# Windowed attention with sinks, then a normalised two-layer network: the first layer's Strassen half from the fourth chunk on, and a new order of loads

## The chip, the cores and the metric

The kernel runs on one core of one Trainium2 chip. The metric is the device time of one execution in microseconds, as the median of several runs. A profiled execution has a span, from its first to its last instruction, and a time of its own, which is a little longer.

## What is computed

Four sequences of 768 positions with 8 heads of 64 go through attention in which a position sees the first 4 positions (sinks) and the last 128 positions. The result, 512 values for each position, is normalised, goes through two matrix products with a relu between them, and is added to the result of the attention.

```
scores = q @ k.T / sqrt(64)                      # batch 4, heads 8, seq 768, head_dim 64
keep   = (pos_k < 4) | (0 <= pos_q - pos_k < 128)
a      = softmax(where(keep, scores, -1e9))
x      = (a @ v) heads side by side              # [4, 768, 512]
xn     = (x - mean(x)) / sqrt(var(x) + 1e-6) * g_ln
out    = x + relu(xn @ w_ch1) @ w_ch2            # w_ch1 512 x 2048, w_ch2 2048 x 512
```

## The kernel before

The 3072 positions are cut into 24 tiles of 128 (t) and 12 chunks of two tiles (c); three chunks make a sequence. Weights and activations are held in bf16, sums in fp32.

Nothing is ordered by hand. `Plan` collects operations (`P.op(name, engines, priority, ...)`), each with its possible engines and an assumed duration, what it reads and writes, and a priority that reads as a due time: the smaller goes first. `Plan.run` is a list scheduler: it takes the engine on which something can start first, and of the operations that can start there within a small window (0.2 to 0.25 us) the one of the smallest priority. `nb` is a time before which an operation does not start. Operations of TensorE with a priority of 40 or more (`strict`) go in the order of their priorities; those below go as they become ready. The planned order is then the program of each engine, and each engine runs it in order. Where the plan leaves TensorE idle in the first 24 us, filler matmuls on a tile `junk` are put in (L1236).

The numbers are in the dictionary `PAR`. For chunk c, `at(c, step)` is `16 c - 8 + PAR[step]`, and for chunks above `PAR["half"]` the offsets come from the inner dictionary `h` (L555).

What a chunk goes through:

- Loads. q, k and v come through GpSimd's (POOL's) DMA queue, with at most eight loads in flight: a load waits for the one eight before it. Chunks 1 to 3 load k and q as one tile each (`load4`, L602, tiles n4a to n4c) and transpose them on TensorE (L672); later chunks load by tile (L687) and transpose by DMA on SP's queue (L569). The v tiles come by `load_v` (L589), the four quarters of w1 by `w1ld` (L547) and of w2 by `w2ld` (L550). All of them can be issued from the start, so their priorities alone (`w1p`, `w2p`, `vp`, `ld1`, and `tr` less 14 from chunk 3 on) set the order.
- Attention. Scores on TensorE (L754, L802), exponentials on ScalarE (ACT, L758, L814), a mask product on VectorE (DVE, L826) or for some of the later chunks on POOL (L821, `mkp`), the sinks' values (L721; `vs0` for the first batch, L707), the product with v (L854), and the division and normalisation on DVE and POOL (L868 to L885). The normalised rows `xc` are transposed into `xnt`, from chunk 2 on by DMA.
- First layer. `mlp` forms eight groups `ph` of hidden units, each 8 matmuls with 256 columns (L1027; in chunks 0 and 1 by tile, 16 matmuls with 128 columns, L1020), followed by a relu (L1037). A chunk uses w1 quarter `u // 2` for group u. From chunk `PAR["half"]` on, groups 0 to 3 are formed by `halves` instead: seven products of 8 matmuls with 128 columns (L958), after Strassen. Their right sides are four sums of `xnt` made on POOL (L938, due `T - tlead`), their left sides w1 itself and four sums of w1 (`weight_sums`, L923, due `wsum`). Three products are copied out by ACT (`snap`, L969) and added to others by DVE (`total`, L980), and relus follow (L983, L1001).
- Second layer. Chunks 0 and 1: four steps of 4 matmuls with 512 columns for each tile, with the quarters 0 to 3 of w2 in this order (L1058). From chunk 2 on `wino` makes it by seven products of 8 matmuls with 256 columns (L1109), with sums of the hidden units (L1092), sums of w2 (L1178), and DVE adding the residual (L1123, L1130).

After chunk 1 the w1 quarters are multiplied by g_ln in place (L1190), before chunk 2 uses them.

Of the kernel before, what the change touches and what calls it, by code (L numbers as in the profile page):

```python
# [64 lines left out]
class Plan:  # L65
# [49 lines left out]
    def run(self):  # L115
# [8 lines left out]
        while ready:  # L124
# [5 lines left out]
            for o in ready:  # L130
                if "PE" in o.engs and o is not head and o.prio >= PAR["strict"]:
                    continue
# [44 lines left out]
            else:  # L177
# [6 lines left out]
                else:  # L184
# [22 lines left out]
def pe(us):  # L207
    return {"PE": (us, us + Plan.PE_DRAIN)}
# [28 lines left out]
NEG = -1e30  # L237
NEVER = -1e9

PAR = dict(split=(3, 4, 5, 6, 7), gsum=-8.0, guard=183.0, strict=40.0, win=0.4, tr=-8.0, sc=-5.3, sc1=-2.0, av=2.0, trx=9.0, by_dma=4, x_by_dma=2, g_on_w=2, av2=20.0, avi=1.0, behind=5, gtt=9.0, ramp=0.3, vs0=2.6, vpb=12.0,  # L240
           w1p=(0.15, 1.7, 2.05, 2.8), pm=2, w2p=(4.5, 4.51, 4.52, 4.53), by_tile=2, wino=2, vp=(0.0, 0.1, 2.0, 2.1, 4.2, 4.3), ld1=0.05,
           h=dict(av=1.62, avi=0.4, sc=-7.53, sc1=-3.14, tr=-20.67, trx=9.0, xo=-11.34), mkp=(0,), mko=-3.48, vsp=1, soon=0, lb=0, xlag=2.1, llag=2.4, mix=(1.0, 0.5), tzp=16.19, kp=-0.9, half=4, wsum=58.0, flip=1, te=("POOL",), tlead=33.28, rd=0, cpr=20.34, sp=(10.74, 5.73), sq=(-5.24, -23.14, 6.14, 23.93), pos=(0.11, 1.67, 2.3, 8.33, 1.63, 2.3, 3.91), pos4=(7.29, 3.8, 1.67, 7.72))


def general(tc, nc, slots, pairs, ones, ident_f, ident, w1, w2, mhalf, g_s, g_r, q, k, v, out, scale):


    V, A, G, T, DMA = nc.vector, nc.scalar, nc.gpsimd, nc.tensor, nc.gpsimd.dma_start
    B, H, S, D = q.shape
# [14 lines left out]
    def transposes(src, dst):  # L264
        for a in range(HP):
            T.transpose(ones[0][:, 128 * a:128 * a + 128], src[:, 128 * a:128 * a + 128], ident_f)
        A.copy(flat(dst), ones[0])

    with tc.For_i(0, B, 1) as b:
        DMA(ks_n[0:NS].rearrange("s (h d) -> s h d", h=H), k[b, :, 0:NS, :].rearrange("h s d -> s h d"))  # L270
        DMA(vs_n[0:NS].rearrange("s (h d) -> s h d", h=H), v[b, :, 0:NS, :].rearrange("h s d -> s h d"))
# [102 lines left out]
def kernel(  # L374
# [87 lines left out]
    Bw1, Bw1g = [Buf(f"w1_{c}") for c in range(4)], [Buf(f"w1g_{c}") for c in range(4)]  # L462
# [42 lines left out]
    def negs(e):  # L505
# [405 lines left out]
    wsum, xt_b = [], {}  # L911

    def weight_sums():
        a = [w1[m][:, 2 * i:2 * i + 2, :] for m in range(2) for i in range(2)]
        get = {n: (lambda i=i: a[i]) for i, n in enumerate(("a11", "a12", "a21", "a22"))}
        held = [Buf(f"ws{i}", "hq") for i in range(2)]
        for i, (x0, x1, op) in enumerate((("a21", "a22", ALU.add), (0, "a11", ALU.subtract),
                                          ("a11", "a21", ALU.subtract), ("a12", 1, ALU.subtract))):
            done = Buf(f"wsum{i}")
            ap = lambda i=i: held[i // 2].t[:, 2 * (i % 2):2 * (i % 2) + 2, :]  # L920
            val = lambda x: ap(x) if isinstance(x, int) else get[x]()
            P.op(f"wsum{i}", {"DVE": dve(1024, 0.52)}, PAR["wsum"] + 3.0 * i, lambda e, ap=ap, x0=x0, x1=x1, op=op, val=val:
                 V.tensor_tensor(ap(), val(x0), val(x1), op=op), reads=Bw1g[0:2] + [wsum[x][1] for x in (x0, x1) if isinstance(x, int)],  # L923
                 hold=[held[i // 2]], writes=[done], nb=PAR["wsum"] + 3.0 * i)
            wsum.append((ap, done, held[i // 2]))

# [79 lines left out]
    def mlp(c):  # L1006
# [36 lines left out]
        if c >= PAR["wino"]:  # L1043
            return wino(c, T, hq, h1, quick)
# [27 lines left out]
                     reads=[ot, oo], dma=HW_S)  # L1072

    def wino(c, T, hq, h1, quick):
        A = [lambda g=g: hq[g].t.rearrange("p (v k) (s t) -> p k v s t", k=2, s=2) for g in range(2)]
        part = {"a11": lambda g: A[g]()[:, 0, :, :, 0:128], "a21": lambda g: A[g]()[:, 0, :, :, 128:256],
                "a12": lambda g: A[g]()[:, 1, :, :, 0:128], "a22": lambda g: A[g]()[:, 1, :, :, 128:256]}
        if quick:
            h1 = [None] * 4 + h1
        deps = {n: [quick[int(n[1]) - 1] if quick and g == 0 else h1[4 * g + (0 if n[2] == "1" else 1)::2][:2] for g in range(2)] for n in part}  # L1080
        sb = {}

        def get(n, g):
# [2 lines left out]
        def need(n, g):  # L1086
            return [sb[n, g]] if n[0] == "s" else deps[n][g]
        for i, (n, x0, x1, op) in enumerate((("s3", "a11", "a21", ALU.subtract), ("s1", "a21", "a22", ALU.add),
                                             ("s2", "s1", "a11", ALU.subtract), ("s4", "a12", "s2", ALU.subtract))):
            for g in range(2):  # L1090
# [3 lines left out]
                    reads=need(x0, g) + need(x1, g), writes=[sb[n, g]], hold=[hq[g]])  # L1094
# [56 lines left out]
        for half in (0, 2, 3, 1) if c == NC - 1 else (0, 1) if c in PAR["split"] else ():  # L1151
            t, sl = 2 * c + half // 2, slice(256 * (half % 2), 256 * (half % 2) + 256)
# [3 lines left out]
        for i in () if c == NC - 1 else (1,) if c in PAR["split"] else (1, 0):  # L1156
            t = 2 * c + i
# [16 lines left out]
    for qt in range(4):  # L1174
        b11, b12, b21, b22 = (w2[qt][:, 2 * i:2 * i + 2, 256 * j:256 * j + 256] for i in range(2) for j in range(2))
        t1, t2, t3, t4 = (w2t[i][:, qt] for i in range(4))
        for i, (o, x0, x1) in enumerate(((t1, b12, b11), (t2, b22, t1), (t3, b22, b12), (t4, b21, t2))):
            P.op(f"w2t{i}_{qt}", {"DVE": dve(512, 0.52)}, 16.0 * PAR["wino"] - 6.0 + qt + 0.1 * i, lambda e, o=o, x0=x0, x1=x1: V.tensor_tensor(  # L1178
                o, x0, x1, op=ALU.subtract), reads=[Bw2[qt]] + ([Bw2t[i - 1][qt]] if i in (1,) else [Bw2t[1][qt]] if i == 3 else []),
                writes=[Bw2t[i][qt]], after=idle[i])  # L1180

    for c in range(NC):
# [3 lines left out]
        if c == PAR["g_on_w"] - 1:  # L1186
            for s in range(4):
                for j in range(NDM):
                    P.op(f"w1g{s}{j}", {"DVE": fix(0.36), "ACT": (0.61, 0.72)}, 16.0 * c + 11.0 + 2 * s + 0.1 * j,
                         lambda e, s=s, j=j: (V.tensor_scalar_mul if e == "DVE" else nc.scalar.mul)(  # L1190
                             w1[s][:, j, :], w1[s][:, j, :], gt[:, j:j + 1]),
                         reads=[Bw1[s], Bc["gt"]], writes=[Bw1g[s]], after=last_use[s])

    def guard(e):
# [8 lines left out]
         reads=[pt_f], writes=[fl_b])  # L1203
# [76 lines left out]
```

## Time and profile before

| | |
|---|---|
| median of three runs | 208.49 us (208.41 to 209.63) |
| the profiled execution's own time | 208.16 us |
| its span | 206.6 us |
| busy: TensorE / weight loads / DVE / ACT / POOL | 199.4 / 165.6 / 179.6 / 119.7 / 118.7 us |
| granted TensorE clock | 1.000 |
| bytes moved by DMA | 27.55 MB |

The page names engines PE (TensorE matmul), PEld (TensorE weight load), DVE, ACT, POOL and SP. In a group's line stand the code line, engine, operation, tiles written and read, shapes and count; behind the bar the busy time in us, the mean of one in ns, and behind the second bar idle time of the engine just before, with what ended it. In a timeline a row has start, duration, engine, line, operation and count, and in brackets the idle time before it. A row of stretches has start and end, its length, and the busy time of PE, PEld, DVE, ACT and POOL with the number of instructions, then clock, share of the DMA engines and GB/s.

### The profile page before, as it was taken

The page shows a single profiled execution, that of the slowest core. Times are in us where ns is not written, and L with a number is a line of the kernel's source. Part 1 is how long each engine was busy: PE and PEld are TensorE (multiplying, and loading weights), DVE is VectorE, ACT ScalarE, POOL GpSimd, SP SyncE. Part 2 cuts the span into 40 slices and gives each one's busy share as a digit, 9 for nine tenths or more (in the row PEclk, how much of TensorE's full clock was granted, in tenths as well). Part 3 has the DMA queues.
Part 4 walks back from the last instruction along what each step waited for, and adds up shares of the span by engine and source line. Part 5 has one row for each costly group of instructions (what it writes and reads, how often), then busy time and mean ns, then how long its engine had stood idle before and what let it go on. Part 6 is the DMA issues. An engine that isn't in the chain of part 4 may idle for free.

```text
span 206.6 us, 6790 instructions
## 1 busy us (share of the span) xinstructions
PE 199.4 (97%) x2766; PEld 165.6 (80%) x2766; DVE 179.6 (87%) x437; ACT 119.7 (58%) x187; POOL 118.7 (57%) x170
## 2 busy tenths in 40 slices
PE   6888999999999999999999999999999999999994
PEld 2557996674698897898998988988988988988993
DVE  7589769899599899899989989989989989998693
ACT  3649477839555655666486486485486585560620
POOL 7977475279039029959649949968627229125000
PEclk9999999999999999999999999999999999999999
DMA  5999999999999999999999999899976411210302
GB/s 117 146 195 195 197 181 205 199 158 171 186 200 124 124 191 101 121 174 101 175 152 137 113 159 143 109 171 114 194 117 101 128 33 23 106 32 19 108 27 84
DMA packets 101341, 27.55 MB, mean 133 GB/s; under 512 B 89652, under 2 KB 99128, under 8 KB 101304
## 3 DMA queue, kind: packets, MB, share of 16 engines
q0 software_dynamic: 67712, 13.37, 81.7%
q1 hardware_dynamic: 33304, 13.43, 34.1%
q8 instruction: 22, 0.36, 0.7%
q10 hardware_dynamic: 288, 0.26, 0.4%
q14 instruction: 15, 0.12, 0.2%
HBM read 27.31 MB, written 6.29 MB: 163 GB/s over the span
## 4 chain that ended last, share of the span: by engine, by line
PE 90%; DMA 3%; DVE 3%; POOL 2%; issue 0%; DVEq 0%
PE one L1109 31%; PE one L1027 20%; PE one L958 12%; PE one L1058 7%; PE one L1020 7%; PE pair L854 5%; PE pair L802 4%; DMA n4b<-in_q_dram 3%; PE one L672 1%; PE pair L721 1%; POOL nat L626 1%; PE one L714 1%; DVE xnt L907 1%; DVE kq L595 1%; POOL vn L589 0%; DVE st L874 0%
## 5 line engine op out<-in xcount | busy, mean ns | idle before, releaser
L1027 PE MATMUL one<-xnt,w 128*128 128x256 bf16 x384 | 46.8, 273 | 0.0
L814 ACT ACTIVATE pe<-pair 128x1024 bf16<-128x1024 f32 (+1 forms) x40 | 36.3, 963 | 18.2 <-PE pair L802 18.2
L1037 ACT ACTIVATE hq<-one 128x512 bf16<-128x512 f32 x58 | 33.4, 590 | 17.9 <-PE one L1020 9.4
L1027 PEld LDWEIGHTS <-w 128*128 128x128 bf16 x384 | 36.3, 98 | 4.0
L1109 PEld LDWEIGHTS <-hs 128*128 128x128 bf16 x320 | 31.0, 98 | 4.0
L882 POOL TENSOR_SCALAR st<-st 128x1 f32<-128x1 f32 x24 | 6.4, 266 | 44.4 <-DVE rec L868 27.5
L826 DVE TENSOR_TENSOR pe<-pe,mask 128x1024 bf16<-128x1024 bf16 (+1 forms) x35 | 27.1, 799 | 1.6 <-ACT pe L814 1.4
L969 ACT COPY tz<-one 128x512 f32<-128x512 f32 x24 | 13.9, 585 | 20.6 <-PE one L958 19.2
L1109 PEld LDWEIGHTS <-hq 128*128 128x128 bf16 x240 | 22.2, 98 | 4.1 <-issue 0.5
L589 POOL DMA_DIRECT2D vn<-in_v_dram x24 | 21.9, 922 | 2.2 <-DMA w<-in_moe_w_ch_dram 1.2
L983 ACT ACTIVATE hq<-hq 128x512 bf16<-128x512 bf16 x24 | 15.1, 630 | 13.1 <-DVE hq L980 12.6
L1109 PE MATMUL one<-w,hq 128*128 128x256 bf16 x160 | 19.2, 273 | 0.0
L980 DVE TENSOR_TENSOR hq<-one,tz 128x512 bf16<-128x512 f32 x24 | 16.4, 684 | 1.9 <-PE one L958 1.0
L1130 DVE TENSOR_TENSOR ot<-one,tm 128x256 f32<-128x256 f32 x40 | 15.9, 412 | 2.1 <-PE one L1109 1.8
L1123 DVE TENSOR_TENSOR tm<-one,x 128x256 f32<-128x256 f32 x40 | 16.6, 414 | 1.2 <-PE one L1109 1.1
L870 DVE TENSOR_TENSOR x<-pair,rec 128x512 bf16<-128x512 f32 x24 | 16.6, 691 | 0.8
L874 DVE BATCH_NORM_STATS2 st<-x 128x6 f32<-128x512 bf16 x24 | 16.5, 687 | 0.2
L1020 PE MATMUL one<-xnt,w 128*128 128x128 bf16 x256 | 16.0, 219 | 0.5 <-DVE xnt L907 0.5
L687 POOL DMA_DIRECT2D nat<-in_q_dram x16 | 14.2, 893 | 3.7 <-DMA w<-in_moe_w_ch_dram 3.7
L938 POOL TENSOR_TENSOR xt<-xnt 128x256 bf16<-128x256 bf16 x16 | 12.2, 778 | 7.1 <-DMA xnt<-xc 7.0
L687 POOL DMA_DIRECT2D nat<-in_k_dram x16 | 14.8, 928 | 2.4 <-DMA w<-in_moe_w_ch_dram 2.4
L1020 PEld LDWEIGHTS <-w 128*128 128x128 bf16 x256 | 14.6, 98 | 1.6 <-issue 0.8
(130 smaller groups left out, 387.7 us busy)
## 6 DMA issues: line engine op xcount, KB each, us to landing
out_dram<-ot SPq DMA_DIRECT2D x17, 256.0 KB
w<-in_moe_w_ch_dram POOLq DMA_DIRECT2D x8, 512.0 KB, 12.8
vn<-in_v_dram POOLq DMA_DIRECT2D x24, 128.0 KB, 6.9
nat<-in_k_dram POOLq DMA_DIRECT2D x17, 128.0 KB, 4.6
nat<-in_q_dram POOLq DMA_DIRECT2D x17, 128.0 KB, 4.9
out_dram<-ot SPq DMA_DIRECT2D x14, 128.0 KB
kq<-nat SPq DMA_TRANSPOSE x32
xnt<-xc SPq DMA_TRANSPOSE x20
```

The lines of the kernel that those rows point to most:

```text
L589: loads[b * RB + r, "v"] = P.op(f"vld{t}", {"POOL": (0.87, 0.9)}, prio, lambda e: G.dma_start(bv.t[:, :, 0:64], v[b, :, 128 * r:128 * (r + ...
L687: lambda e, nat=nat, ap=ap: G.dma_start(nat.t, ap), writes=[nat], dma=SW if c < 6 else (*SW[:2], PAR["llag"]), after=behind(c, 0 if soon e ...
L814: P.op(f"ex{c}{hp}", {"ACT": act(2 * n)}, d + 0.1 + 0.05 * j, lambda e, pp=pp, pb=pb: nc.scalar.activation(pb.t[:, :, 0:n], pp.t[:, :, 0:n ...
L826: V.tensor_mul(pb.t[:, :, 0:n], pb.t[:, :, 0:n], mm),
L870: P.op(f"x{t}", {"DVE": dve(512)}, d + xo + 0.11, lambda e: V.tensor_tensor(x.t.rearrange("p (a h c) -> p a h c", a=2, c=64), pv()[:, :, : ...
L874: P.op(f"bn{t}", {"DVE": fix(0.60)}, d + xo + 0.12, lambda e: V.bn_stats(st.t[:, 8:14], x.t), reads=[x], writes=[st, mv])
L958: nc.tensor.matmul(b.t[:, 128 * h:128 * h + 128], lhsT=lt[:, kk, 128 * h:128 * h + 128], rhs=rh[:, kk, :], start=first and h == 0 and kk = ...
L1020: nc.tensor.matmul(ph.t[:, 128 * s:128 * s + 128], lhsT=w1[u // 2][:, j, 128 * s:128 * s + 128], rhs=xnt.t[:, j, 128 * (u % 2):128 * (u % ...
L1027: nc.tensor.matmul(ph.t[:, 256 * s:256 * s + 256], lhsT=w1[ht // 4][:, j, 128 * (ht % 4):128 * (ht % 4 + 1)], rhs=xnt.t[:, j, :], start=j ...
L1037: nc.scalar.activation(hg.t[:, u % 4, :], ph.t, AF.Relu)
L1109: nc.tensor.matmul(at(r), lhsT=get(left, g)[:, v, s, :], rhs=rhs, start=first and n == 0, stop=n == 7, skip_group_check=True)
L1123: return P.op(f"tm{name}_{c}", {"DVE": dve(256, 1.14)}, pr - PAR["kp"], lambda e: V.tensor_tensor(tm[name].t, at(r), xs[i].t[:, sl], op=AL ...
```

## The change

`half` goes from 4 to 3, so chunk 3 too forms the first half of its hidden units by `halves`, and the offsets of `h` hold from chunk 4 on instead of chunk 5. Nearly all due times in `PAR` are other numbers, those of the loads of w1, w2, v and chunk 1's k and q among them. The four sums of w1 may go to POOL as well as to DVE, at an assumed 2.8 us. The due time of the w2 sums gets a name, `w2tp`, of the value that it had (16 x 2 - 6 = 26). In `wino` a second layout of the hidden units is added for chunks below `by_tile`, which is 2, as is the first chunk of `wino`.

```
-PAR = dict(split=(3, 4, 5, 6, 7), ..., tr=-8.0, sc=-5.3, sc1=-2.0, av=2.0, ..., av2=20.0, ..., vs0=2.6, vpb=12.0,
-           w1p=(0.15, 1.7, 2.05, 2.8), pm=2, w2p=(4.5, 4.51, 4.52, 4.53), by_tile=2, wino=2, vp=(0.0, 0.1, 2.0, 2.1, 4.2, 4.3), ld1=0.05,
-           h=dict(av=1.62, avi=0.4, sc=-7.53, sc1=-3.14, tr=-20.67, trx=9.0, xo=-11.34), mkp=(0,), mko=-3.48, ..., tzp=16.19, kp=-0.9, half=4, wsum=58.0, ..., tlead=33.28, rd=0, cpr=20.34, sp=(10.74, 5.73), sq=(-5.24, -23.14, 6.14, 23.93), pos=(0.11, 1.67, 2.3, 8.33, 1.63, 2.3, 3.91), pos4=(7.29, 3.8, 1.67, 7.72))
+PAR = dict(we=('DVE', 'POOL'), w2tp=26.0, split=(3, 4, 5, 6, 7), ..., tr=-15.61, sc=-15.19, sc1=-9.67, av=-7.15, ..., av2=10.16, ..., vs0=-1.95, vpb=12.0,
+           w1p=(1.98, 3.22, 1.69, 2.84), pm=2, w2p=(5.17, 3.68, 6.24, 5.48), by_tile=2, wino=2, vp=(-3.05, 1.66, 2.16, 2.51, 10.26, 9.11), ld1=-2.61,
+           h=dict(av=1.5, avi=0.4, sc=-8.28, sc1=-3.3, tr=-16.85, trx=9.0, xo=-14.56), mkp=(0,), mko=-12.81, ..., tzp=13.3, kp=-0.5, half=3, wsum=47.41, ..., tlead=40.63, rd=0, cpr=53.87, sp=(7.12, 11.19), sq=(-1.28, -1.95, 6.81, 38.9), pos=(0.11, 1.66, 2.1, 6.95, 1.5, 1.93, 3.95), pos4=(5.08, 3.61, 1.84, 5.95))
...
-            P.op(f"wsum{i}", {"DVE": dve(1024, 0.52)}, PAR["wsum"] + 3.0 * i, lambda e, ...:
-                 V.tensor_tensor(ap(), val(x0), val(x1), op=op), ...
+            P.op(f"wsum{i}", {e: dve(1024, 0.52) if e == "DVE" else fix(2.8) for e in PAR["we"]}, PAR["wsum"] + 3.0 * i, lambda e, ...:
+                 (V if e == "DVE" else G).tensor_tensor(ap(), val(x0), val(x1), op=op), ...
...
     def wino(c, T, hq, h1, quick):
-        A = [lambda g=g: hq[g].t.rearrange("p (v k) (s t) -> p k v s t", k=2, s=2) for g in range(2)]
...
+        if c < PAR["by_tile"]:
+            A = [lambda g=g: hq[g].t.rearrange("p (v t) (k s n) -> p t k v s n", t=2, k=2, s=2) for g in range(2)]
...
+        else:
+            A = [lambda g=g: hq[g].t.rearrange("p (v k) (s t) -> p k v s t", k=2, s=2) for g in range(2)]
...
-            P.op(f"w2t{i}_{qt}", {"DVE": dve(512, 0.52)}, 16.0 * PAR["wino"] - 6.0 + qt + 0.1 * i, ...
+            P.op(f"w2t{i}_{qt}", {"DVE": dve(512, 0.52)}, PAR["w2tp"] + qt + 0.1 * i, ...
```

More of the change, by code (lines that the diff above doesn't have):

```diff
@@ L238 @@
 NEVER = -1e9
-PAR = dict(split=(3, 4, 5, 6, 7), gsum=-8.0, guard=183.0, strict=40.0, win=0.4, tr=-8.0, sc=-5.3, sc1=-2.0, av=2.0, trx=9.0, by_dma=4, x_by_dma=2, g_on_w=2, av2=20.0, avi=1.0, behind=5, gtt=9.0, ramp=0.3, vs0=2.6, vpb=12.0,
-           w1p=(0.15, 1.7, 2.05, 2.8), pm=2, w2p=(4.5, 4.51, 4.52, 4.53), by_tile=2, wino=2, vp=(0.0, 0.1, 2.0, 2.1, 4.2, 4.3), ld1=0.05,
-           h=dict(av=1.62, avi=0.4, sc=-7.53, sc1=-3.14, tr=-20.67, trx=9.0, xo=-11.34), mkp=(0,), mko=-3.48, vsp=1, soon=0, lb=0, xlag=2.1, llag=2.4, mix=(1.0, 0.5), tzp=16.19, kp=-0.9, half=4, wsum=58.0, flip=1, te=("POOL",), tlead=33.28, rd=0, cpr=20.34, sp=(10.74, 5.73), sq=(-5.24, -23.14, 6.14, 23.93), pos=(0.11, 1.67, 2.3, 8.33, 1.63, 2.3, 3.91), pos4=(7.29, 3.8, 1.67, 7.72))
+PAR = dict(we=('DVE', 'POOL'), w2tp=26.0, split=(3, 4, 5, 6, 7), gsum=-8.0, guard=183.0, strict=40.0, win=0.4, tr=-15.61, sc=-15.19, sc1=-9.67, av=-7.15, trx=9.0, by_dma=4, x_by_dma=2, g_on_w=2, av2=10.16, avi=1.0, behind=5, gtt=9.0, ramp=0.3, vs0=-1.95, vpb=12.0,
+           w1p=(1.98, 3.22, 1.69, 2.84), pm=2, w2p=(5.17, 3.68, 6.24, 5.48), by_tile=2, wino=2, vp=(-3.05, 1.66, 2.16, 2.51, 10.26, 9.11), ld1=-2.61,
+           h=dict(av=1.5, avi=0.4, sc=-8.28, sc1=-3.3, tr=-16.85, trx=9.0, xo=-14.56), mkp=(0,), mko=-12.81, vsp=1, soon=0, lb=0, xlag=2.1, llag=2.4, mix=(1.0, 0.5), tzp=13.3, kp=-0.5, half=3, wsum=47.41, flip=1, te=("POOL",), tlead=40.63, rd=0, cpr=53.87, sp=(7.12, 11.19), sq=(-1.28, -1.95, 6.81, 38.9), pos=(0.11, 1.66, 2.1, 6.95, 1.5, 1.93, 3.95), pos4=(5.08, 3.61, 1.84, 5.95))
 def general(tc, nc, slots, pairs, ones, ident_f, ident, w1, w2, mhalf, g_s, g_r, q, k, v, out, scale):
@@ L921, in weight_sums @@
             val = lambda x: ap(x) if isinstance(x, int) else get[x]()
-            P.op(f"wsum{i}", {"DVE": dve(1024, 0.52)}, PAR["wsum"] + 3.0 * i, lambda e, ap=ap, x0=x0, x1=x1, op=op, val=val:
-                 V.tensor_tensor(ap(), val(x0), val(x1), op=op), reads=Bw1g[0:2] + [wsum[x][1] for x in (x0, x1) if isinstance(x, int)],
+            P.op(f"wsum{i}", {e: dve(1024, 0.52) if e == "DVE" else fix(2.8) for e in PAR["we"]}, PAR["wsum"] + 3.0 * i, lambda e, ap=ap, x0=x0, x1=x1, op=op, val=val:
+                 (V if e == "DVE" else G).tensor_tensor(ap(), val(x0), val(x1), op=op), reads=Bw1g[0:2] + [wsum[x][1] for x in (x0, x1) if isinstance(x, int)],
                  hold=[held[i // 2]], writes=[done], nb=PAR["wsum"] + 3.0 * i)
@@ L1074, in wino @@
     def wino(c, T, hq, h1, quick):
-        A = [lambda g=g: hq[g].t.rearrange("p (v k) (s t) -> p k v s t", k=2, s=2) for g in range(2)]
-        part = {"a11": lambda g: A[g]()[:, 0, :, :, 0:128], "a21": lambda g: A[g]()[:, 0, :, :, 128:256],
-                "a12": lambda g: A[g]()[:, 1, :, :, 0:128], "a22": lambda g: A[g]()[:, 1, :, :, 128:256]}
+        if c < PAR["by_tile"]:
+            A = [lambda g=g: hq[g].t.rearrange("p (v t) (k s n) -> p t k v s n", t=2, k=2, s=2) for g in range(2)]
+            part = {f"a{t + 1}{k + 1}": (lambda g, t=t, k=k: A[g]()[:, t, k]) for t in range(2) for k in range(2)}
+        else:
+            A = [lambda g=g: hq[g].t.rearrange("p (v k) (s t) -> p k v s t", k=2, s=2) for g in range(2)]
+            part = {f"a{t + 1}{k + 1}": (lambda g, t=t, k=k: A[g]()[:, k, :, :, 128 * t:128 * t + 128]) for t in range(2) for k in range(2)}
         if quick:
             h1 = [None] * 4 + h1
-        deps = {n: [quick[int(n[1]) - 1] if quick and g == 0 else h1[4 * g + (0 if n[2] == "1" else 1)::2][:2] for g in range(2)] for n in part}
+        deps = {n: [quick[int(n[1]) - 1] if quick and g == 0 else h1[4 * g + int(n[1 if c < PAR["by_tile"] else 2]) - 1::2][:2] for g in range(2)] for n in part}
         sb = {}
@@ L1177 @@
         for i, (o, x0, x1) in enumerate(((t1, b12, b11), (t2, b22, t1), (t3, b22, b12), (t4, b21, t2))):
-            P.op(f"w2t{i}_{qt}", {"DVE": dve(512, 0.52)}, 16.0 * PAR["wino"] - 6.0 + qt + 0.1 * i, lambda e, o=o, x0=x0, x1=x1: V.tensor_tensor(
+            P.op(f"w2t{i}_{qt}", {"DVE": dve(512, 0.52)}, PAR["w2tp"] + qt + 0.1 * i, lambda e, o=o, x0=x0, x1=x1: V.tensor_tensor(
                 o, x0, x1, op=ALU.subtract), reads=[Bw2[qt]] + ([Bw2t[i - 1][qt]] if i in (1,) else [Bw2t[1][qt]] if i == 3 else []),
```

## The prediction

> **What bounds the kernel now.** I read the page first, then TensorE's waits, then the stretches of time, then the spacing of the products inside one chunk.
>
> ```profile
> span 206.6 us, 6790 instructions
> PE 199.4 (97%) x2766; PEld 165.6 (80%) x2766; DVE 179.6 (87%) x437; ACT 119.7 (58%) x187; POOL 118.7 (57%) x170
> ```
>
> TensorE (PE) is busy for 199.4 of 206.6 us. The stretches (start:end, then busy us of PE, PEld, DVE, ACT, POOL) say where the missing 7.2 us are, and the waits of PE in the first 24 us say on whom:
>
> ```profile
> 10.00:12.00 2.00, 1.81 (x23) 0.98 (x22) 1.22 (x3) 0.19 (x1) 1.55 (x3) 1.00 1.77 178
> 12.00:14.00 2.00, 1.40 (x43) 1.21 (x38) 1.51 (x4) 1.17 (x2) 1.28 (x3) 1.00 1.32 204
> 14.00:16.00 2.00, 1.84 (x40) 1.22 (x38) 1.97 (x4) 1.64 (x2) 1.22 (x3) 1.00 1.24 204
> 16.00:18.00 2.00, 1.88 (x40) 1.67 (x41) 1.90 (x5) 1.86 (x4) 1.71 (x3) 1.00 1.60 192
> 18.00:20.00 2.00, 1.55 (x28) 1.24 (x27) 2.00 (x5) 2.00 (x4) 1.49 (x3) 1.00 1.47 198
> 20.00:22.00 2.00, 2.00 (x43) 1.77 (x41) 1.93 (x5) 0.90 (x2) 0.67 (x1) 1.00 1.68 188
> 45.00:50.00 5.00, 5.00 (x63) 2.80 (x60) 4.88 (x16) 4.70 (x8) 4.81 (x8) 1.00 2.14 181
> 50.00:60.00 10.00, 10.00 (x97) 7.01 (x95) 7.80 (x17) 5.42 (x9) 2.32 (x4) 1.00 2.06 178
> 60.00:70.00 10.00, 10.00 (x138) 8.44 (x136) 9.20 (x23) 6.09 (x9) 6.50 (x8) 1.00 1.44 138
> 200.00:207.00 7.00, 3.60 (x34) 2.90 (x31) 3.12 (x9) 0.00 (x0) 0.00 (x0) 0.96 0.24 81
> ```
>
> ```profile
> PE pair L854 <- ACT pe L758: 0.9, 1, 0.9
> PE one L672 <- DMA n4b<-in_q_dram: 0.6, 1, 0.6
> PE one L1020 <- DVE xnt L907: 0.5, 1, 0.5
> ```
>
> From 20 us to the last product PE has no idle time: two stages are shown full, and the rest of the stretches read the same. So a transfer, a wait or an order inside 20 to 200 us can hardly be made better by the change; only fewer or shorter matmuls shorten it. It can be made worse. Gains from order are left for the first 20 us and the 3.4 us of the tail, which this diff does not touch in kind.
>
> **The Strassen half of the fourth chunk.** `half` goes from 4 to 3, so chunk 3 forms hidden units 0 to 1023 by seven products of eight 128-column matmuls instead of four groups of eight 256-column matmuls. Chunk 4 of the same trace does the first form beside the second, so the starts give both prices:
>
> ```profile
> 86.56 0.61 PE L958 MATMUL one<-xt,hq 128*128 128x128 bf16 x8
> 87.01 0.61 PE L958 MATMUL one<-xnt,w 128*128 128x128 bf16 x8
> 87.46 1.04 PE L1027 MATMUL one<-xnt,w 128*128 128x256 bf16 x8
> 88.33 0.65 PE L854 MATMUL pair<-vn,pe 128*128 128x65 bf16 x16
> ...
> L1027 PE MATMUL one<-xnt,w 128*128 128x256 bf16 x384 | 46.8, 273 | 0.0
> L958 PE MATMUL one<-xt,hq 128*128 128x128 bf16 x192 | 14.6, 219 | 0.0
> ```
>
> From 86.56 to 87.01 and from 87.01 to 87.46 are 0.45 us for eight short matmuls; from 87.46 to 88.33 are 0.87 us for eight long ones. Seven products cost 7 x 0.45 = 3.15 us, four groups 4 x 0.87 = 3.48 us: PE is relieved of 0.33 us. The last two rows price it otherwise, by busy time: 14.6 / 192 = 76 ns and 46.8 / 384 = 122 ns, so 56 x 0.076 = 4.26 against 32 x 0.122 = 3.90 us, a loss of 0.36 us. Busy time includes the tail of each group's last matmul (0.61 us are shown for a group that the next follows after 0.45 us), so I take the starts: -0.33, with +0.36 as the other end.
>
> A rule of the Trainium skill speaks against this part: TensorE: Matmul & The Clock Gate, section Back-to-back issue gap, says that a stream which reloads weights for every matmul runs at about 81 ns per 128-column matmul, well above the isolated 56 ns. By it seven products would cost an estimated 56 x 81 ns = 4.5 us, and the part would lose 1.1 us against the row's 3.48 us. The trace disagrees: 0.45 us for eight is 56 ns each, weights reloaded each time.
>
> What chunk 3 adds elsewhere, by these rows (groups of lines, the last with its shapes apart):
>
> ```profile
> L980 DVE TENSOR_TENSOR hq<-one,tz 128x512 bf16<-128x512 f32 x24 | 16.4, 684 | 1.9 <-PE one L958 1.0 <-ACT tz L969 0.4
> L969 ACT COPY tz<-one 128x512 f32<-128x512 f32 x24 | 13.9, 585 | 20.6 <-PE one L958 19.2 <-DVE ot L1130 0.6 <-DVE rec L868 0.6
> L938 POOL TENSOR_TENSOR xt<-xnt,xt 128x256 bf16<-128x256 bf16 x16 | 13.6, 851 | 0.6
> L923 DVE TENSOR_TENSOR hq<-w 128x1024 bf16<-128x1024 bf16 x1 | 0.7, 685 | 0.0
> L826 DVE TENSOR_TENSOR pe<-pe,mask 128x1024 bf16<-128x1024 bf16 x23 | 20.4, 908 | 0.7 <-ACT pe L814 0.7
> ```
>
> DVE gets three sums of 0.684 (+2.05 us), ACT three copies of 0.585 (+1.76 us; the four relus stay four), POOL four sums of activations at up to 0.85 (+3.4 us). In exchange the first mask product of chunk 4 (0.91 us) goes from DVE to POOL, since the rules for later chunks now hold from chunk 4 on. None of these three engines is full between 60 and 70 us (DVE 9.20, ACT 6.09, POOL 6.50 of 10), and the four sums of weights (4 x 0.685 = 2.74 us) leave that stretch for an earlier one. The loads of chunk 5 stand behind the POOL sums on their queue, a whole chunk ahead of their use. Cost on the path: nothing, as long as PE has chunk 2's second layer to do meanwhile; without that cover the 2.05 us would be late for PE. Two edits do nothing: the sums of w2 keep their due time (26 is 16 x 2 - 6), and the new branch of the second layer's Strassen serves chunks below 2, which never call it.
>
> **The sums of weights.** They carry a due time of 47.4 instead of 58 us and may run on POOL, where the planner counts 2.8 us each; the nearest row, four times 0.851, gives 3.4 us. Between 45 and 60 DVE is busy 4.88 + 7.80 = 12.68 of 15 us. With 2.74 us of weight sums it would be full (15.4), and the earlier attention of chunk 3 adds its evictions there too. So some of it slides past 60 or goes to POOL, which does only 2.32 us in 50 to 60. The first product that needs a sum starts in chunk 3, about 1.4 us after 69.5 us. That is nine us of cover: 0.
>
> **The loads.** All loads are on POOL's queue, eight in flight. Before, by priority: k, q of tile 1, v0, k and q of chunk 1, v1, w1 quarters 0 and 1, v2, w1 2, v3, w1 3, k and q of chunk 2, v4, v5, w2 0, 1, 2, 3, k and q of chunk 3. After: the same six, then w1 2 and 0, v2, v3, w1 3 and 1, w2 1, k and q of chunk 2, w2 0, 3, 2, v5, v4, k and q of chunk 3. Waits for a free place show when quarters land:
>
> ```profile
> 16.13 0.96 POOL L589 DMA_DIRECT2D vn<-in_v_dram  x1 [0.75 <-DMA w<-in_moe_w_ch_dram]
> 18.93 0.96 POOL L589 DMA_DIRECT2D vn<-in_v_dram  x1 [0.49 <-DMA w<-in_moe_w_ch_dram]
> 22.07 0.74 POOL L550 DMA_DIRECT2D w<-in_moe_w_ch_dram  x1 [1.40 <-DMA w<-in_moe_w_ch_dram]
> 32.85 0.87 POOL L687 DMA_DIRECT2D nat<-in_k_dram  x1 [0.85 <-DMA w<-in_moe_w_ch_dram]
> 35.28 0.87 POOL L687 DMA_DIRECT2D nat<-in_k_dram  x1 [1.55 <-DMA w<-in_moe_w_ch_dram]
> 38.67 0.87 POOL L687 DMA_DIRECT2D nat<-in_q_dram  x1 [2.52 <-DMA w<-in_moe_w_ch_dram]
> 40.73 0.88 POOL L687 DMA_DIRECT2D nat<-in_q_dram  x1 [1.19 <-DMA w<-in_moe_w_ch_dram]
> 39.89 1.13 PE L854 MATMUL pair<-vn,pe 128*128 128x65 bf16 x32
> 44.45 3.59 SPq L569 DMA_TRANSPOSE xnt<-xc  x2
> 54.34 1.91 PE L1027 MATMUL one<-xnt,w 128*128 128x256 bf16 x16
> ```
>
> The first weights are the seventh load in both orders and land by 16.1 us; nothing ahead of them moved, so PE's waits up to then (0.9 for an exponential, 0.6 for chunk 1's q) stay. Which quarter comes first does not matter, since any quarter gives the ready tile its hidden units. After that a quarter lands every 2.1 to 3.4 us and feeds two chunks: four groups of 0.87, 3.5 us of PE. PE stays the slower of the two. The first quarter of w2 that the output products need (quarter 0; the four are added in order) lands near 32.8 now; ahead of it stands one quarter more (2.6 us, the mean of the last three intervals) and two v tiles less (each a quarter of such a load's size: about 0.65 us, an estimate), so near 34.1, while chunk 1's first layer still has matmuls to run. Cost 0.
>
> The v tiles of chunk 2 move past four quarters and are the last before chunk 3's keys. The same bytes have then landed as at 40.7, so both are there near 40.7 and the value products, at 39.89 now, start at 41. Their normalised rows are transposed at 44.45 to 48.04 and first used at 54.34; if the landing takes as long again as the two issues, 3.6 us (an estimate), there are 2.7 us of cover against 1.1 us of delay. Cost 0, and 1.6 us of room. The scores of chunks 2 and 3 are now due before the first chunks' products, but start no earlier than their keys and queries land, and those stand behind one quarter more.
>
> **The start.**
>
> ```profile
> L707 DVE TENSOR_TENSOR vs<-one,sel 128x260 bf16<-128x260 f32 x1 | 0.4, 422 | 0.0
> 15.34 0.50 PE L1236 MATMUL one<-junk 128*128 128x512 bf16 x3
> ```
>
> Bounds: at best the idle of 12 to 20 us goes (8.00 - 1.40 - 1.84 - 1.88 - 1.55 = 1.33 us) and with it the last filler matmuls (0.50 us); at worst the sink values of batch 0 (0.42 us on DVE, priority now ahead of the rest) delay the chain that the 0.5 us wait at L1020 ends. I take 0: the six first loads and the chain of tiles 0 to 3 are unchanged, and a second quarter has landed by 18.9 for PE to use meanwhile. From chunk 5 on the products keep their order on PE (I sorted the priorities of both versions: the attention steps fall between the same products), so there too 0.
>
> **Sum.** 208.16 us of this profiled execution (206.6 of span and 1.56 around it) - 0.33 = 207.8. The median of the three runs is 208.49, 0.33 above the profiled one, so the forecast on the median is 208.49 - 0.33 = 208.2 us: no change beyond 1%, which is about what a measurement of this kernel can tell from none.
>
> **The rivals.** (1) *v comes too late for chunk 2*: if the two v tiles land later than 42.6 us (39.89 and the 2.7 of cover), because w2's last quarters and chunk 3's keys share the transfers with them, chunk 2's first layer has no input, and PE stops where it now never does. At two loads of a quarter's pace later, 40.7 + 2 x 2.6 = 45.9, PE stops for 3.3 us: 211.5. For it: each w2 quarter is waited for on the queue today. Against it: the orders end with the same bytes. (2) *DVE between 45 and 70 us*: the weight sums and the new sums, 2.74 + 2.05 = 4.8 us, meet a DVE that has 2.3 us free in 45 to 60. It decides when what slides past 60 is not absorbed by the room that the weight sums leave there: 4.8 - 2.3 = 2.5 us late for PE, 210.7. Against it: 0.8 us are free in 60 to 70 and 2.74 come free. (3) *Short products don't pay*: +0.36, 208.9. (4) *The start gains all it can*: -1.33 - 0.50 - 0.33 = -2.16: 206.3. Against it: more than half of that idle time ends before the first weights land at 16.1.
>
> **Chances.** Forecast 0.56; short products dear 0.04; v late 0.18; DVE full 0.15; start gains 0.07. Within 1% are the first two, 0.60; slower 0.33; faster 0.07. The range leaves out the start's full gain and the worst of the v case: 206.9 to 211.2; the forecast's own is 207.3 (half the start's gain) to 209.3 (+0.36 and +0.42).
>
> **What would show it.** L958 grows from 448 to 504 matmuls and L1027 falls from 384 to 352, at the same 0.45 and 0.87 us between starts. PE's stretches from 20 to 200 us stay full: if one shows a gap at the first L1027 of chunk 2 (near 54 us), released by a DMA into xnt, rival 1 is right; a gap at 69 to 75 us released by DVE, or an L923 on POOL over 3.4 us, is rival 2. If 12 to 20 us fill up, rival 4. A change of more than 2 us either way with PE full throughout would mean that the pricing by starts is wrong.

## The result, and the profile after

The changed kernel takes 217.44 us (median; 214.66 to 218.96), the kernel before 208.63 in the same measurement: a ratio of 1.0363 [1.029, 1.0437]. The forecast was 208.2, the range 206.9 to 211.2. In what follows ratios are over the undisturbed executions alone; the profiled execution of the first experiment is one of its longer ones, so its waits are read and not its total.

The head of the page of the changed kernel's profiled execution (217.34 us), and the group of the first layer's long products:

```profile
span 215.8 us, 6845 instructions
PE 203.3 (94%) x2786; PEld 167.7 (78%) x2793; DVE 184.5 (85%) x436; ACT 121.7 (56%) x192; POOL 124.1 (58%) x177
...
L1027 PE MATMUL one<-xnt,w 128*128 128x256 bf16 x352 | 43.0, 273 | 0.0
```

The span is 9.2 us longer. The long products fell to 352, as announced. TensorE's share went from 97% to 94%. The waits of TensorE (us in total, times, longest) name a new releaser at their head:

```profile
PE pair L802 <- DMA kq<-nat: 4.5, 4, 1.5
```

L802 are scores; they wait for keys or queries that SP's queue transposes by DMA (L569). TensorE's timeline shows the places (chunks 4, 6 and 8), the stretches what follows the first of them:

```profile
63.56 0.25 PE L802 MATMUL pair<-kq,kq 64*64 64x64 bf16 x4 [0.76 <-DMA kq<-nat]
64.82 0.33 PE L802 MATMUL pair<-kq 64*64 64x192 bf16 x8 [1.01 <-DMA kq<-nat]
...
98.59 0.51 PE L802 MATMUL pair<-kq 64*128 64x256 bf16 x8 [1.29 <-DMA kq<-nat]
...
130.76 0.33 PE L802 MATMUL pair<-kq 64*64 64x192 bf16 x8 [1.48 <-DMA kq<-nat]
```

```profile
62.00:64.00 2.00, 1.05 (x12) 0.69 (x10) 1.80 (x6) 1.16 (x2) 0.84 (x1) 1.00 1.28 261
64.00:66.00 2.00, 1.18 (x33) 0.86 (x33) 0.36 (x1) 0.80 (x1) 2.00 (x4) 0.96 1.28 308
66.00:68.00 2.00, 2.00 (x11) 1.44 (x10) 0.91 (x2) 1.31 (x3) 2.00 (x3) 0.50 2.18 162
68.00:70.00 2.00, 2.00 (x15) 1.54 (x14) 2.00 (x2) 0.00 (x0) 2.00 (x4) 0.69 2.42 144
```

From 62 to 66 TensorE is busy for 2.23 of 4 us, and then it is "busy" at a granted clock of 0.50 and 0.69: 2 x 0.50 + 2 x 0.31 = 1.6 us more are lost though no wait is shown. A busy row therefore has to be read with its clock. The half clock is not part of every execution: two of the six, at 216.59 and 214.66 us, show a mean clock of 1.000, the others 0.992.

Another 1.3 us lie ahead of chunk 2's first layer. The first of the normalised rows' copies on DVE (L907) stands behind the sinks' values (L707) now, and the first product of the first layer starts at 17.50 instead of 16.68. Most of this lateness lies ahead of the sinks' values: the copy before them (L595) starts at 14.05 instead of 13.41, behind the transposes (L672) that wait for chunk 1's q. The first product of chunk 2, at 54.34 before, starts at 55.66:

```profile
14.05 1.23 DVE L595 COPY kq<-one 128x1024 bf16<-128x1024 bf16 x1 [0.60 <-PE one L672]
15.19 0.42 DVE L707 TENSOR_TENSOR vs<-one,sel 128x260 bf16<-128x260 f32 x1
15.53 0.68 DVE L907 TENSOR_TENSOR xnt<-one,gt 128x512 bf16<-128x512 bf16 x1
...
17.50 1.07 PE L1020 MATMUL one<-xnt,w 128*128 128x128 bf16 x16
...
55.66 1.58 PE L1027 MATMUL one<-xnt,w 128*128 128x256 bf16 x13
```

Some 1.8 us of the 9.2 are left in smaller pieces that were not followed.

Why a transpose is late can be read on SP's queue. Chunk 8's in the changed kernel, and the same step before:

```profile
118.81 3.81 SPq L569 DMA_TRANSPOSE kq<-nat  x3
122.71 0.54 SPq L1162 DMA_DIRECT2D out_dram<-ot  x1
123.34 2.67 SPq L569 DMA_TRANSPOSE kq<-nat  x1
```

```profile
112.78 5.47 SPq L569 DMA_TRANSPOSE kq<-nat  x4
118.34 0.53 SPq L1159 DMA_DIRECT2D out_dram<-ot  x1
```

Before, four transposes (two tiles of keys, two of queries) go out in a row and the store of an older chunk follows. Now that store stands ahead of the fourth: from the first transpose's start to the end of the last one's issue it takes 7.20 us (118.81 to 126.01) instead of 5.47, and the score that needs it waits until 130.76. `tr` went from -20.67 to -16.85, past the due time of the store.

The store needs a result of DVE, but here it did not wait for it: its issue starts 0.09 us after the third transpose's ends (122.62 to 122.71), and so it does in chunk 6 (91.08 to 91.17). Where it did wait, for 6.5 us in chunk 5, no score waited:

```profile
64.33 3.94 SPq L569 DMA_TRANSPOSE kq<-nat  x3
74.72 0.33 SPq L1162 DMA_DIRECT2D out_dram<-ot  x1
```

In chunk 4 the first of the two waits ends when the second transpose lands (63.52), which stands ahead of the store, so that one is not the store's.

### The profile page after: what moved, and what is told of

It reads as the page before. It is cut to its first block, busy times and chain, and to the rows that moved or that the text cites. A ratio compares the mean times of both kernels' runs of the same rounds, so it can differ in the third digit from the quotient of the medians.

```text
span 215.8 us, 6845 instructions
## 1 busy us (share of the span) xinstructions
PE 203.3 (94%) x2786; PEld 167.7 (78%) x2793; DVE 184.5 (85%) x436; ACT 121.7 (56%) x192; POOL 124.1 (58%) x177
## 5 line engine op out<-in xcount | busy, mean ns | idle before, releaser
L1027 PE MATMUL one<-xnt,w 128*128 128x256 bf16 x352 | 43.0, 273 | 0.0
L1037 ACT ACTIVATE hq<-one 128x512 bf16<-128x512 f32 x56 | 32.0, 589 | 10.7 <-PE one L1027 6.2
L1027 PEld LDWEIGHTS <-w 128*128 128x128 bf16 x352 | 33.3, 98 | 3.6
L969 ACT COPY tz<-one 128x512 f32<-128x512 f32 x27 | 15.7, 585 | 24.5 <-PE one L958 23.1
L826 DVE TENSOR_TENSOR pe<-pe,mask 128x1024 bf16<-128x1024 bf16 (+1 forms) x34 | 28.2, 857 | 0.7 <-ACT pe L814 0.7
L1112 PEld LDWEIGHTS <-hq 128*128 128x128 bf16 x240 | 22.7, 100 | 4.7 <-issue 0.5
L983 ACT ACTIVATE hq<-hq 128x512 bf16<-128x512 bf16 x27 | 17.0, 630 | 15.1 <-DVE hq L980 14.4
L1112 PE MATMUL one<-w,hq 128*128 128x256 bf16 x160 | 20.6, 285 | 0.0
L980 DVE TENSOR_TENSOR hq<-one,tz 128x512 bf16<-128x512 f32 x27 | 18.5, 684 | 2.0 <-PE one L958 1.2
L958 PEld LDWEIGHTS <-hq 128*128 128x128 bf16 x288 | 17.3, 98 | 0.2
L938 POOL TENSOR_TENSOR xt<-xnt 128x256 bf16<-128x256 bf16 x18 | 13.5, 767 | 6.4 <-PE one L1112 3.1
L958 PE MATMUL one<-xt,hq 128*128 128x128 bf16 x216 | 16.5, 219 | 0.0
```

The source lines that it names most:

```text
L826: V.tensor_mul(pb.t[:, :, 0:n], pb.t[:, :, 0:n], mm),
L958: nc.tensor.matmul(b.t[:, 128 * h:128 * h + 128], lhsT=lt[:, kk, 128 * h:128 * h + 128], rhs=rh[:, kk, :], start=first and h == 0 and kk = ...
L980: o = P.op(f"c{n}_{c}", {"DVE": dve(512, 1.14)}, pr, lambda e: V.tensor_tensor(block(n), banks_[bank].t.rearrange("p (i t) -> p i t", i=4) ...
L983: P.op(f"r{n}_{c}", {"ACT": act(512), "DVE": dve(512, 0.26)} if PAR["rd"] else {"ACT": act(512)}, pr + 0.1, lambda e: nc.scalar.activation ...
L1027: nc.tensor.matmul(ph.t[:, 256 * s:256 * s + 256], lhsT=w1[ht // 4][:, j, 128 * (ht % 4):128 * (ht % 4 + 1)], rhs=xnt.t[:, j, :], start=j ...
L1037: nc.scalar.activation(hg.t[:, u % 4, :], ph.t, AF.Relu)
```

## The experiments

**The store goes back behind the fourth transpose.** One number in the changed kernel; TensorE, DVE, ACT and POOL keep their orders:

```
-  h=dict(..., tr=-16.85, ...)
+  h=dict(..., tr=-20.67, ...)
```

> The changed kernel with one number put back: h.tr from -16.85 to -20.67. In the program this moves one thing, on SP's queue: in each of the chunks 4 to 11 one store of a finished tile goes from ahead of the chunk's fourth key/query transpose to behind it (8 moves, every other engine's order is the same). Theory A (a store that waits for a late DVE sum holds up the fourth transpose, so the scores wait): PE's 4.5 us of waits for kq by DMA go, and with the first of them the stretch of 66 to 69 us at half clock (about 1.7 us): 217.4 - 5.3 - 1.7 = 210.4 us, between 209.5 and 212. Rival B (DVE is full and late by itself): the waits go over into waits for DVE sums, 214 to 217. Rival C (keys and queries come too late by their loads, whatever the queue): no change, 216 to 218.

211.83 us, ratio 1.0086 [1.0041, 1.0131]. From 1.0363, 2.8% of the time or about 5.7 us come from the place of one store on SP's queue, in each of eight chunks. SP's and TensorE's rows:

```profile
117.44 5.14 SPq L569 DMA_TRANSPOSE kq<-nat  x4
122.67 1.98 SPq L1162 DMA_DIRECT2D out_dram<-ot  x1
```

```profile
PE pair L802 <- DMA kq<-nat: 1.3, 2, 0.7
PE one L672 <- issue: 1.2, 1, 1.2
PE pair L854 <- DMA vn<-in_v_dram: 0.7, 1, 0.7
```

The waits at 98 and 130 us are gone, those of chunk 4 are shorter, and the clock stays at 1.00. Of 4.5 us of waits 3.2 went, with the 1.6 us of half clock; about 1 us is left that no wait names. Of theory A the place of the store is shown, its wait for a late DVE sum is not: in chunks 6 and 8 of the changed kernel there was none. What stands between the third and the fourth transpose there is the store's issue and its transfer: in chunk 8 the DMA packets of the third end at 123.40, those of the store (128 of 2048 bytes) run from 123.75 to 126.60, those of the fourth from 125.38 to 128.00. The fourth lands 11.9 us after the first one's start there, and 8.8 us in this kernel.

**The same alone, on the kernel before** (`tr` from -20.67 to -16.85, which puts the store ahead in chunks 5 to 11).

> The mirror: the kernel before with h.tr from -20.67 to -16.85 and nothing else. Only SP's order changes: in chunks 5 to 11 a store comes ahead of the fourth transpose, as in the changed kernel. Theory A: PE gets waits for kq, fewer than in the changed kernel since DVE is less late here: 210 to 213 us against 208.6. Rivals B and C: no change, 208 to 209.

211.42 us, ratio 1.0099 [1.0048, 1.015]: slower, but less than half of what undoing it gained. The trace has only 0.5 us of waits for transposes. Of the 2.1 us by which its span is longer, 0.5 lie ahead of chunk 2's first product, where this edit changes no order; the rest builds up between 80 and 190 us:

```profile
PE pair L802 <- DMA kq<-nat: 0.5, 2, 0.3
```

So it confirms the sign, not the size. In both kernels TensorE is ready for the scores of chunks 6 and 8 that need the fourth transpose 10.3 to 10.5 us after the first transpose's start. The fourth lands 10.4 and 10.6 us after that start in this kernel, 11.7 and 11.9 us in the changed one; what takes the 1.3 us more there is not shown.

**The Strassen half of chunk 3 alone, on the kernel before.**

```
-  half=4, wsum=58.0
+  half=3, wsum=47.41
```

> The kernel before with the Strassen half from chunk 3 on (half 3, sums of w1 due at 47.4) and nothing else; loads, due times and sums of the hidden units as before. On SP's queue the fourth transpose of chunk 4 moves ahead of a store. Theory A and my pricing by starts: -0.33 us, 208.0 to 208.8. Rival D (the Strassen half in chunk 3 overloads DVE or POOL, or short products don't pay): 209.5 to 212.

209.16 us, ratio 1.0017 [0.9985, 1.0048]. The change that gives this case its name costs nothing that can be measured. Where chunk 3's second layer begins, its price can be read (this kernel, then before):

```profile
78.19 1.05 PE L1109 MATMUL one<-w,hq 128*128 128x256 bf16 x8
```

```profile
78.61 0.61 PE L1109 MATMUL one<-w,hq 128*128 128x256 bf16 x4
```

It begins 0.42 us earlier, 0.36 of it won since the chunk's first product (69.49 and 69.55), where -0.33 was forecast; further on these tenths are lost again.

**The order of the loads alone, on the kernel before.**

```
-  w1p=(0.15, 1.7, 2.05, 2.8), w2p=(4.5, 4.51, 4.52, 4.53), vp=(0.0, 0.1, 2.0, 2.1, 4.2, 4.3), ld1=0.05
+  w1p=(1.98, 3.22, 1.69, 2.84), w2p=(5.17, 3.68, 6.24, 5.48), vp=(-3.05, 1.66, 2.16, 2.51, 10.26, 9.11), ld1=-2.61
```

> The kernel before with the order of the loads of w1, w2, v and chunk 1's k and q of the changed kernel and nothing else. Theory A: what the first 55 us lost is small, 208.5 to 209.8. Rival C (late loads make the loss): 211 or more, with PE waits for w or vn before 60 us.

213.97 us, ratio 1.0254 [1.0163, 1.0345]. That is more than theory A allowed. TensorE stops at the first product of chunk 2's first layer:

```profile
31.71 1.08 PE L672 MATMUL one<-ident,n4c 128*64 128x128 bf16 x32
...
44.86 1.14 PE L854 MATMUL pair<-vn,pe 128*128 128x65 bf16 x32
...
55.92 0.27 PE L1027 MATMUL one<-xnt,w 128*128 128x256 bf16 x1 [1.66 <-DMA xnt<-xc]
```

```profile
48.89 3.60 SPq L569 DMA_TRANSPOSE xnt<-xc  x2
```

Before, the first of these rows is:

```profile
29.05 1.08 PE L672 MATMUL one<-ident,n4c 128*64 128x128 bf16 x32
```

Chunk 2's keys and queries (n4c) stand behind one quarter of w2 more and are transposed 2.66 us later. Together with the later v tiles that puts the value products at 44.86 instead of 39.89, and the normalised rows' transposes at 48.89 instead of 44.45. Of the 4.0 us by which this trace's span is longer, 1.6 are lost by this product; the rest builds up later, without a wait over 0.5 us.

**The two v tiles alone, and the quarters alone, on the kernel before.** The first sets only the last two values of `vp` to (10.26, 9.11). The second takes all of the new order except these two, which stay ahead of w2's last quarters:

```
+  vp=(0.0, 0.1, 2.0, 2.1, 10.26, 9.11)
```

```
+  w1p=(1.98, 3.22, 1.69, 2.84), w2p=(5.17, 3.68, 6.24, 5.48), vp=(-3.05, 1.66, 2.16, 2.51, 4.8, 4.9), ld1=-2.61
```

> The kernel before with only the v tiles of chunk 2 due later (10.26 and 9.11 instead of 4.2 and 4.3), so that they are loaded behind the four quarters of w2. If the v tiles are what costs in the new load order (my rival 1 in the prediction): PE waits some 2 us at the first L1027 of chunk 2, released by a DMA into xnt, 210 to 213. If not: 208 to 209.5.

> The complement: the kernel before with the new order of the weight quarters, of v 0 to 3 and of chunk 1's k and q, but the v tiles of chunk 2 ahead of three quarters of w2, as they nearly are in the kernel before. If the v tiles are the cost: 208 to 209.5 and no wait at the first L1027. If the order of the weights is: 211 or more.

The v tiles alone: 210.21 us, 1.0052 [1.0022, 1.0083]. The quarters alone: 210.91 us, 1.0079 [1.0051, 1.0107], with most of the wait at chunk 2:

```profile
PE pair L854 <- DMA vn<-in_v_dram: 0.6, 1, 0.6
```

```profile
PE one L1027 <- DMA xnt<-xc: 1.5, 1, 1.5
```

```profile
43.90 1.14 PE L854 MATMUL pair<-vn,pe 128*128 128x65 bf16 x32
```

The first row is of the v tiles alone, the others of the quarters alone, where the value products start 4.0 us later than before. So the late keys make the gap, not the v tiles. Together they cost more (2.5%) than in sum (1.3%). A part of that can be the clock: with both, three of four executions show a mean clock of 0.989 to 0.992, and the fourth, at 0.998, takes 212.31 us; of the two parts alone, every execution shows 0.998 to 1.000.

**The loads of before in the changed kernel, without and with the store's place of before.**

> The changed kernel with the loads (w1p, w2p, vp, ld1) of the kernel before; the stores still ahead of the fourth transposes. Theory A+C (two causes: the store ahead of the transpose, and the order of the loads): the load part goes, the store part stays: 212 to 214.5. If the loads were only bad in the company of the old due times: no change, 216 to 218.

> The changed kernel with both put back: the loads of the kernel before, and h.tr -20.67 (stores behind the fourth transposes). Strassen in chunk 3, the sums of w1, the late fourth sums of the hidden units and all other due times as in the changed kernel. Theory A+C: what is left is within 1% of before, 208 to 210. Rival B (the DVE sums, due later in the changed kernel, cost by themselves): 211 or more, with PE waits for hs.

217.56 us, 1.0392 [1.0334, 1.045], and 215.41 us, 1.0306 [1.0259, 1.0353]. The expected gain from the loads did not come: something else takes 6 us. The waits of the second one, then DVE and POOL at that place:

```profile
PE pair L854 <- DVE pe L826: 3.6, 4, 1.6
```

```profile
49.12 4.37 DVE L1181 TENSOR_TENSOR w2t<-w,n4c 128x512 bf16<-128x512 bf16 x1
...
53.76 1.01 DVE L826 TENSOR_TENSOR pe<-pe,mask 128x768 bf16<-128x768 bf16 x2
```

```profile
49.26 1.80 POOL L589 DMA_DIRECT2D vn<-in_v_dram  x2
51.02 2.18 POOL L923 TENSOR_TENSOR hq<-w 128x1024 bf16<-128x1024 bf16 x1
```

A subtraction on DVE that takes 0.4 us elsewhere takes 4.37 (4.38 in the first of the two kernels), and it ends 0.3 us after POOL's weight sum (53.49 and 53.20). Behind it stand chunk 3's mask products (L826), for which TensorE waits 3.6 us; after that its clock is 0.54 and 0.60 from 58 to 62 us. This was not in any forecast: with before's loads the planner puts the first weight sum, not the second, on POOL, beside two-input work of DVE.

**All weight sums on DVE.** Against the kernel just shown only the first sum moves, from POOL to DVE:

```
-  we=('DVE', 'POOL')
+  we=('DVE',)
```

> The changed kernel with the loads and the key/query transposes due as before (215.4 in the earlier run), and now with all four sums of w1 on DVE; only the first of them moves, from POOL to DVE. Theory (POOL's sum holds back DVE): in the earlier run one 128x512 subtraction on DVE with two inputs took 4.37 us while POOL ran its sum, and PE then waited 3.6 us for mask products and ran at half clock for 4 us (about 1.8 us). Without a sum on POOL that subtraction takes 0.4 us, the 3.6 us and the half clock are gone, and the time is 215.4 - 3.6 - 1.8 = 210.0 (209.3 to 211). Rival (the w2 subtractions simply stand ahead of the mask products on DVE): 215.4 or up to 0.7 more, since DVE now has one sum more.

210.88 us, ratio 1.0102 [1.0067, 1.0137]: 4.5 us less, 210.0 forecast. The same stretch of DVE and POOL:

```profile
48.77 0.42 DVE L1181 TENSOR_TENSOR w2t<-w,n4c 128x512 bf16<-128x512 bf16 x1
...
49.44 1.03 DVE L826 TENSOR_TENSOR pe<-pe,mask 128x768 bf16<-128x768 bf16 x2
```

```profile
49.61 1.79 POOL L589 DMA_DIRECT2D vn<-in_v_dram  x2
```

The same subtraction takes 0.42 us, the two mask products run beside POOL's same two DMA issues in 1.03 us, and TensorE's wait for L826 is gone: it was the sum that held DVE. The Trainium skill, SBUF — State Buffer, section SBUF: two separate sides, says that GpSimd and DVE share a pair of ports under an exclusive lock, that a DVE operation with two inputs in SBUF needs it against a GpSimd operation that reads SBUF, and that the later one is blocked for the other's whole length. These runs agree, with two things beside it. The hold lasted longer than the 2.18 us shown for the sum and began 1.9 us ahead of it; the records do not say why. And the changed kernel itself escapes it: its sum on POOL runs from 55.59 for 2.12 us beside DVE operations that each keep their usual length, among them this one, with two inputs of which one is the f32 result of TensorE:

```profile
55.59 2.12 POOL L923 TENSOR_TENSOR hq<-hq,w 128x1024 bf16<-128x1024 bf16 x1 [0.52 <-DVE rec L868]
...
55.59 0.69 DVE L870 TENSOR_TENSOR x<-pair,rec 128x512 bf16<-128x512 f32 x1
```

**Due times of the hidden-unit sums and of the sinks' values too.** `sp`, `sq` and `vs0` of before, on top of the last kernel; and, in another kernel, `sp` and `sq` of before on top of the first experiment:

```
+  sp=(10.74, 5.73), sq=(-5.24, -23.14, 6.14, 23.93), vs0=2.6
```

> As the run with all sums of w1 on DVE, and also with the due times of the hidden-unit sums (sp, sq) and of the first sinks' values (vs0) as before. What is left of the change is the Strassen half in chunk 3 and the earlier due times of scores and value products. Theory: these two cost the 0.4 us of vs0 at the start and up to 0.7 us from 150 us on, so 208.6 to 209.4, the time of before. Rival (the earlier attention costs of itself, by what it puts ahead of other work on DVE and ACT): 210 or more.

> The changed kernel with the key/query transposes due as before (211.8 in the earlier run) and the hidden-unit sums (sp, sq) due as before. DVE's order alone differs. Theory: the late sum costs little once the stores do not stand ahead of the transposes: the earlier run lost 0.7 us against before from 160 us on, so 211.1 to 211.8. Rival (late sums on DVE are a main cost): 209.5 or less.

211.2 us, 1.011 [1.0069, 1.0152], and 213.68 us, 1.0224 [1.0176, 1.0272]. Both miss. The sinks' values and the sums are not what was left, and in the second kernel the sums of before cost 1.4% instead of gaining: its waits for transposes are 2.6 us against 1.3, with SP's order the same. Why the transposes landed later there was not settled.

**One mask product.** What both kernels with before's loads share is this, shown for the one with all sums on DVE:

```profile
67.27 1.29 POOL L938 TENSOR_TENSOR xt<-xnt 128x256 bf16<-128x256 bf16 x2 [2.61 <-DMA xnt<-xc]
68.53 1.75 POOL L938 TENSOR_TENSOR xt<-xnt,xt 128x256 bf16<-128x256 bf16 x2
70.23 1.70 POOL L821 TENSOR_SCALAR_AFFINE_SELECT pe<-pe 128x512 bf16<-128x512 bf16 x2
```

```profile
71.39 0.20 PE L854 MATMUL pair<-vn,pe 128*128 128x65 bf16 x1 [0.70 <-POOL pe L821]
71.98 0.63 PE L854 MATMUL pair<-vn,pe 128*128 128x65 bf16 x15 [0.39 <-POOL pe L821]
```

POOL waits 2.61 us for a transpose in order to form sums that are not urgent, and chunk 4's mask product, which `half=3` moves to POOL, stands behind them. It goes back to DVE:

```
-  if R and c > PAR["half"] and hp in PAR["mkp"]:
+  if R and c > PAR["half"] + 1 and hp in PAR["mkp"]:
```

> As the run with all sums of w1 on DVE (210.9), and the one mask product of chunk 4 that half=3 moves to POOL goes back to DVE, as before; nothing else moves. In that run POOL takes the four sums of chunk 3's rows ahead of this mask product and waits 2.6 us there for a DMA, and PE's value product of chunk 4 waits 1.1 us for the mask near 71 us. Theory (this wait is part of what is left): the wait is gone and the time is 210.9 - 1.1 = 209.8 (209.2 to 210.4). Rival (DVE is too full near 70 us, so that the mask comes no earlier or the sums behind it are late): 210.5 or more.

209.32 us, ratio 1.0012 [0.9986, 1.0039]: the time of before. The value products follow without a wait:

```profile
70.64 0.66 PE L854 MATMUL pair<-vn,pe 128*128 128x65 bf16 x16
```

This kernel keeps the Strassen half and all other new due times of the change, and has back the loads, the store's place, one sum and one mask. In this order of steps the 3.63% close in ratios: 2.8% for the store's place (1.0363 to 1.0086), 0.7% for the loads with the sums of w1 and the one mask (1.0086 to 1.0012), and 0.1%, within the error, for all the rest. In another order the shares differ: putting the loads back first gained nothing. None of these versions beats the kernel before.

## Why the prediction was wrong

- *What bounds the kernel* held: between 20 and 200 us order could only make it worse. The steps that then priced the order at nothing failed.
- *"The products keep their order on PE ..., so there too 0"* (from chunk 5 on) is the step that cost most, about 5.7 us. The order was compared on TensorE alone, and there it was indeed the same. `tr` moved a store on SP's queue ahead of the fourth transpose, which lands 2 to 3 us later behind the store's transfer (counted from the first transpose's start, 11.7 instead of 9.7 us in chunk 6 and 11.9 instead of 8.8 in chunk 8); no term of the sum looked at that queue.
- *The loads.* The v tiles were put near 40.7 with 1.6 us of room. In the changed kernel POOL's next loads are released by them at 41.30 and 42.73:

```profile
41.30 0.88 POOL L687 DMA_DIRECT2D nat<-in_q_dram  x1 [0.56 <-DMA vn<-in_v_dram]
42.73 0.87 POOL L687 DMA_DIRECT2D nat<-in_q_dram  x1 [0.55 <-DMA vn<-in_v_dram]
```

  One of them is 2 us later than said. The larger fault is the last sentence of that part: it names that chunk 2's keys and queries stand behind one quarter more, and puts no price on it. The price on the kernel before was 2.66 us at the transposes, 4.0 at the value products and 0.8%, with the v tiles 5.0 and 2.5%. Rival 1 had the place and the sign (chunk 2's first L1027, released by a DMA into xnt) but the wrong cause (v). In the changed kernel itself the gap does not show; what the loads cost there was measured only together with the sums and the mask (0.7%).
- *The weight sums* were costed by lateness alone, with nine us of cover. In the changed kernel that is right: 2.12 us on POOL, below the 3.4 that were to tell of rival 2. What a sum on POOL does to DVE meanwhile was no term; with another order of loads it cost 4.5 us.
- *The first mask product of chunk 4* was counted as a relief of DVE. What stands ahead of it on POOL was not asked, and in the kernels with before's loads that cost 0.9% (1.0102 to 1.0012; 1.6 us between the medians).
- *The start* was taken as 0 between bounds. The bound on the slow side came true: L707 took its 0.42 us ahead of L907. But the first product is 0.82 us later, the copy ahead of both is 0.64 us late already, and with `vs0`, `sp` and `sq` of before the time did not fall (1.0102 and 1.011).
- *The Strassen half* was right, in size too: -0.33 by the starts, 0.36 less measured over the chunk, no effect on the total. Pricing by busy time (+0.36) would have had the wrong sign.
- *The half clock* was in no term. A stall of a kernel that runs at full clock was priced at its own length; that of 62 to 66 us cost nearly as much again in the profiled execution.

## What to carry to other kernels

When due times change, compare the order on every queue, the DMA queues first: a store put ahead of a transfer that TensorE needs makes that transfer late, even where the store itself has nothing to wait for. For a load that moves, follow what it displaces, not only the load itself. Before an operation goes to GpSimd, look at which DVE operations run beside it and what is queued behind it there.

## What the runs showed of the hardware that was not expected

A weight sum of 2.18 us on POOL stretched one DVE operation with two SBUF inputs from 0.42 to 4.37 us, by 3.95 us, nearly twice the sum's own length.

TensorE's clock falls to half after short idle times. In the changed kernel 1.77 us of idle time within 62 to 66 us were followed by half clock until 69 us; the kernel with only the loads changed had one wait of 1.66 us at 54 us and kept 1.00 in its profiled execution. The traces show steps of 3.41 us: each half-clock stretch between 50 and 70 us is that long (65.83 to 69.24 in the changed kernel, 56.85 to 60.26 and 58.18 to 61.59 in the two with before's loads and a sum on POOL) and begins a whole number of such steps after the clock first rose (58.03 or 51.20 us). In the step just ahead of the fall TensorE was idle for 1.77, 2.94 and 1.92 us; the longest idle time in a step without a fall, in any trace here, is 1.75 us (51.35 to 54.77, the last of these kernels). The ends of matmuls are modelled in the profile, so the border is not known to hundredths. The Trainium skill, TensorE: Matmul & The Clock Gate, section What's actually happening, says that the array falls to half rate after one idle window of about 3.4 us and comes back after one busy window of that length. The way back agrees with these runs (from 65.8 to 69.2 us the long products of chunk 2 start 213 ns apart, then 109); the way down does not, since TensorE was busy for nearly half of the step ahead of the fall, and the measurement decides.
